# One pass of an FFN: casts put behind each Relu, a PSUM bank of its own for a temporary, an earlier last fold

## The chip, the core and the metric

The kernel runs on one NeuronCore of a Trainium2 chip. Its engines work side by side, each with a queue of its own that it works through in order: TensorE (PE, with its weight loads shown as PEld), VectorE (DVE), ScalarE (ACT), GpSimd (POOL) and SyncE (SP), which here only issues DMAs. Engines wait for one another by semaphores. The metric is the device time of one execution in microseconds. Before the change the median is 775.13 us, from 3 runs between 774.17 and 776.02.

## The reference

Attention with a few sink tokens and a sliding window, then a Fourier mix over tokens and channels, a normalization and a two-layer FFN:

```python
def _attn_ref(q, k, v, n_sink, window):       # B, H, S, D = 4, 8, 768, 64
    scores = scale * np.matmul(q, k.transpose(0, 1, 3, 2))
    keep = is_sink | in_window                # n_sink = 4, window = 128
    scores = np.where(keep, scores, -1000000000.0)
...
    return np.matmul(a, v).astype(np.float32)

def _moe_ref(x, w_ch1, w_ch2):                # x: 4 x 768 x 512
    X = np.fft.fft(np.fft.fft(x, axis=1), axis=2)
    u = x + np.real(X).astype(np.float32)
    un = (u - mu) / np.sqrt(var + 1e-06)      # over the 512 channels
    ch = np.maximum(un @ w_ch1, 0.0) @ w_ch2  # 512 -> 2048 -> 512
    return (u + ch).astype(np.float32)
```

The FFN weights arrive as 64-bit floats.

## The kernel before

**Precision.** Most matmuls of the transform and the FFN take operands split into two parts: a high part, cast to fp32r by ScalarE, and a low part, the difference, made by DVE (from PSUM) or POOL (from SBUF). Three matmuls then stand for one product: high by high, high by low, low by high. So nearly every tile goes through a cast on ACT and a subtraction on another engine before TensorE may use it.

**Attention and transform.** The tokens are 4 batches of 6 blocks of 128. The attention runs in steps, 4 to a block, with the order of each engine written out by hand (SCHEDULE). When the fourth block of a batch is stored, `fourier` registers the events of that batch's transform: for each of three pairs of blocks j, a fold (`fold_n` adds and subtracts the two blocks, `fold_m` folds the channels, `fold_hi` casts on ACT, `fold_lo` subtracts on DVE; lines 349 to 368), then stage 1 on TensorE (`stage1`, L395: tiles za, zr, zb, with cast L400/L402 and subtraction L407/L410), then stage 2 (`stage2a`, L422, copied from PSUM by ACT at L431; `stage2b`, L443, combined by DVE at L448) and the updates of u (L459, L460). The results of the transform go through two PSUM banks in turn, ps_fft ("fft") and, from the start of the FFN on, ps_n ("n"). F_N, F_M and F_S say how many steps after its blocks are stored a fold's parts are issued, S1 how many steps after the last pair the first stage 1 is issued. For the last batch (`tail`) both parts of a fold are on DVE (FOLD_TAIL).

**The first group's FFN.** The 24 blocks form 6 groups of 4. The first group goes through the FFN while the last batch's transform is still running and while the weights are still being prepared, in the loop over f = 0 to 15 (L1256). For each f:

- `ch1` (L656): 12 matmuls of un by w1's f-th slice of 128 columns, into the PSUM tile h; pool ps_h has two buffers of it. The first two ch1 are issued by events at CH1_AT.
- `split` (L1146, L1147): Relu on ACT, which makes the high half of the hidden tile, and the low half on DVE. Both read h.
- `ch2` of f − 1 (L1154): 12 matmuls into the four output banks.
- `convert` of two weight slices (lines 587 to 626), each in three DVE operations that put a 64-bit float together as fp32 (L599, L600, L601), then a cast on ACT and a subtraction on POOL: L610 and L611 for w1 (tiles tw, w_ring), L624 and L625 for w2 (tiles cv, w). The intermediate w of L599 to L601 is the output tile itself in the first 15 conversions, and later a PSUM tile cw in the bank "fft". The raw slices are loaded by SP (L584), three buffers, a load being issued after the conversion that frees its buffer.
- `combine_w1(p)`, every second f: four sums of quarters of w1's p-th pair on POOL (lines 636 to 639, tile tq), and put off to the next f by the list `late`, the function `halves`: two casts on ACT (L643, tile to), each with a subtraction on POOL (L644), and one DMA that writes the pair to w_dram (L645). tq and to have one buffer.
- from f = 6 on, the second group is normalized and turned (`prepare`: L539, L545, L1199, L1227 to L1238).

When the last batch's transform has ended, its SBUF space becomes the pool "wb" for the later w2 slices.

**The main loop.** Groups 1 to 5 then run with w1 products in Strassen's form (`product`, L1320) into the banks A, B and C, and ch2 at L1348. The banks A and C are the tag "h" of ps_h.

**What sets the order.** Up to step 97 (CUT) and again from L1304 the order of each queue is the order of the code. In between, which is the whole stretch around the change, the framework's planner arranges each engine's queue: it goes by the order of the code, by the dependencies and by its own estimates of how long things take. `tc.issue_after(ins)` adds to it that the instructions of the block, where they are on the engine of `ins`, come behind `ins`.

Of the kernel before, what the change touches and what calls it, by code (L numbers as in the profile page):

```python
# [59 lines left out]
FOLD_AT, FOLD_LAST, FOLD_ENG = (0, 4, 8), (0, 4, 8), "VG"  # L60

F_N, F_M, F_S, ROW = (3, 3), (4, 5), (6, 7), (5, 8, 10)
EV_A = 0

SINK0_AT = 3, 3, "V"
# [71 lines left out]
EV_D, EV_Z = 1, 1  # L137
X_AT, X_NOT = (2,), (81, 97)
SOFT_AT = (0, 1, 2, 3)
S1, S2, UD = 7, 1, 2  # L140
FFT_ORDER = (2, 1, 0)
PARTS = {0: ((2,) * 5, 1, 1), 1: ((2,) * 5, 2, 1), 2: ((2,) * 5, 2, 1)}
PARTS_TAIL = ((1,) * 5, 1, 1)
# [61 lines left out]
def kernel(  # L205
# [65 lines left out]
    def run(general):  # L271
        tag = "g" if general else ""
        with ExitStack() as p1:
# [8 lines left out]
            def at(s, eng, fn):  # L282
                ev.setdefault((s, eng), []).append(fn)
# [49 lines left out]
            def fourier(b, at, ready):  # L333
# [30 lines left out]
                def fold_hi(j):  # L364
                    A.copy(gh[:, j], t_["g", j])

                def fold_lo(j):
                    V.tensor_tensor(gl[:, j], t_.pop(("g", j)), f32(gh[:, j]), op=ALU.subtract)
# [97 lines left out]
                for j in range(NHALF):  # L466
                    k = ready[j]
                    e0, e1 = FOLD_TAIL if tail else FOLD_ENG
                    eng = {"V": V, "G": G}
                    at(k + F_N[0], e0, lambda j=j: fold_n(eng[e0], j, 0))  # L470
                    at(k + F_N[1], e1, lambda j=j: fold_n(eng[e1], j, 1))
                    at(k + F_M[0], e0, lambda j=j: fold_m(eng[e0], j, 0))
                    at(k + F_M[1], e1, lambda j=j: fold_m(eng[e1], j, 1))
                    at(k + F_S[0], "A", lambda j=j: fold_hi(j))
                    at(k + F_S[1], "V", lambda j=j: fold_lo(j))
                at(ready[0] + ROW[0], "V", put_row)
                at(ready[0] + ROW[1], "V", mid_sum)
                at(ready[0] + ROW[2], "V", mid_row)
                k = ready[2] + S1
                n1, na, nb = PARTS_TAIL if tail else PARTS[b]  # L480
                for i, (kind, mc) in enumerate((("a", 0), ("a", 1), ("r", 0), ("b", 0), ("b", 1))):
                    n = n1[i]
# [104 lines left out]
            def convert(i, pool=None):  # L587

                which, f = W_ORDER[i]
                r = raw.pop(i)  # L590
                if which == 0:
                    if f % 2 == 0:
                        state["tw"] = npool.tile([P, 2, 512], I32, tag="tw", name=f"tw{f}", bufs=1 if general else 2)
                    t = state["tw"][:, f % 2]
                else:
                    t = npool.tile([P, 512], I32, tag="qs0", name=f"cv{i}", bufs=QSB)

                w = t if "x" not in state else ps_fft.tile([P, 512], I32, tag="fft", name=f"cw{i}", bufs=1)
                V.tensor_scalar(w, r[:, :, 1], 3, 0x3FFFFFF8, op0=ALU.logical_shift_left, op1=ALU.bitwise_and)  # L599
                V.scalar_tensor_tensor(w, r[:, :, 1], -0x40000000, w, op0=ALU.bitwise_and, op1=ALU.bitwise_or)  # L600
                V.scalar_tensor_tensor(t, r[:, :, 0], 29, w, op0=ALU.logical_shift_right, op1=ALU.bitwise_or)  # L601
                load_w(i + LDB)
                tf = t.bitcast(F32)
                if which == 0:
                    if f == 0:
                        state["ring"] = npool.tile([P, 2, 4, 2, 256], F32R, tag="ring", name="w_ring", bufs=1)
                    fb = state["ring"][:, f // 2 % 2]
                    d = [fb[:, 0:2, j] if f % 2 == 0 else fb[:, 3:1:-1, j] for j in range(2)]
                    tf = tf.rearrange("p (h c) -> p h c", h=2)
                    A.copy(d[0], tf)  # L610
                    G.tensor_tensor(d[1], tf, f32(d[0]), op=ALU.subtract)  # L611
                    Wt[f, 0] = [[d[j][:, cc // 2, P * (cc % 2):P * (cc % 2) + P] for cc in range(NCC)] for j in range(2)]
                    if f % 2 == 1:
                        nc.sync.dma_start(w_dram[f // 2][:, 0:3], f32(fb[:, 0:3]).rearrange("p k s c -> p k (s c)"))
                        state["t", f // 2] = state["tw"].bitcast(F32)
                    return
                if NWA <= f < NWA + NHALF:

                    if f == NWA:
                        state["fold"] = [npool.tile([P, NHALF, DM], F32R, tag=t, name=f"w_{t}", bufs=1) for t in ("gh", "gl")]  # L620
                    d = [t[:, f - NWA] for t in state["fold"]]
                else:
                    d = [pool.tile([P, 512], F32R, name=f"w{f}_{j}") for j in range(2)]
                A.copy(d[0], tf)  # L624
                G.tensor_tensor(d[1], tf, f32(d[0]), op=ALU.subtract)  # L625
                Wt[f, 1] = d
# [3 lines left out]
            def combine_w1(p, pool):  # L630

                t = state.pop(("t", p))
                b11, b21, b12, b22 = t[:, 0, :256], t[:, 0, 256:], t[:, 1, :256], t[:, 1, 256:]
                q = pool.tile([P, 4, 256], F32, tag="tq", name=f"tq{p}")
                o = pool.tile([P, 4, 2, 256], F32R, tag="to", name=f"to{p}")
                G.tensor_tensor(q[:, 1], b12, b11, op=ALU.subtract)
                G.tensor_tensor(q[:, 0], b22, q[:, 1], op=ALU.subtract)  # L637
                G.tensor_tensor(q[:, 2], b22, b12, op=ALU.subtract)
                G.tensor_tensor(q[:, 3], b21, q[:, 0], op=ALU.subtract)  # L639

                def halves():
                    for j in (0, 2):
                        A.copy(o[:, j:j + 2, 0], q[:, j:j + 2])  # L643
                        G.tensor_tensor(o[:, j:j + 2, 1], q[:, j:j + 2], f32(o[:, j:j + 2, 0]), op=ALU.subtract)  # L644
                    nc.sync.dma_start(w_dram[p][:, 3:7], f32(o).rearrange("p k s c -> p k (s c)"))  # L645

                late.append(halves)
# [10 lines left out]
                return ps  # L658

            def start_ffn(s):  # L660
                state["h"] = p1.enter_context(tc.tile_pool(name="ps_h" + tag, bufs=2, space=PSUM))
                banks.append((p1.enter_context(tc.tile_pool(name="ps_n" + tag, bufs=1, space=PSUM)), "n", 1))
                for i in range(LDB):
                    load_w(i)
                for i in range(2):
                    at(s + CONV_AT[i], "V", lambda i=i: convert(i))
                for f in range(2):
                    at(s + CH1_AT[f], "T", lambda f=f: hp.append(ch1(0, f, unT0)))
# [474 lines left out]
            g0 = pg.enter_context(tc.tile_pool(name="g0" + tag, bufs=1, side="right"))  # L1143

            def split(h, x):
                A.activation(h[0], x, AF.Relu)  # L1146
                V.scalar_tensor_tensor(h[1], x, 0.0, f32(h[0]), op0=ALU.max, op1=ALU.subtract)  # L1147

            def ch2(f, h, po):
# [102 lines left out]
            hs = {}  # L1252
            for i in (2, 3):
                convert(i, wa)
            combine_w1(0, g0)
            for f in range(NF):  # L1256
                ps = hp.pop(0) if f < 2 else ch1(0, f, unT0)
                hs[f] = [g0.tile([P, 512], F32R, tag=f"h{i}", name=f"h{i}_{f}", bufs=2) for i in range(2)]
                split(hs[f], ps)
                if pw is None:  # L1260
                    do(1)
                if f > 0:
                    ch2(f - 1, hs.pop(f - 1), po)
                for i in range(2 * f + 4, min(2 * f + 6, 2 * NF)):
                    if i % 2 and pw is None:
                        do(1)
                    if W_ORDER[i][0] == 1 and W_ORDER[i][1] == NWA + NHALF and pw is None:
                        while ev:
                            do(1)
                        pf.close()  # L1270
                        pw = p1.enter_context(tc.tile_pool(name="wb" + tag, bufs=1))
                        state["x"] = [pw.tile([P, 7, 512], F32R, name=f"x{i}") for i in range(2)]
                        state["xf"] = pw.tile([P, 2, NCC, 256], F32, name="xf")
                    convert(i, wa if pw is None else pw)
                while late:
                    late.pop()()
                if f % 2 == 1 and f // 2 + 1 < NPR:
                    combine_w1(f // 2 + 1, g0)
                if f == PREP:
                    steps = prepare(1)  # L1280
                for _ in range(PREP_N if f >= PREP else 0):
                    next(steps, None)
# [21 lines left out]
            with tc.manual_schedule():  # L1304
# [51 lines left out]
                for g in range(1, len(groups)):  # L1356
                    steps = prepare(g + 1) if g + 1 < len(groups) else iter(())
                    for it in range(NIT):
# [10 lines left out]
                        ps = {}  # L1369
                        for k in range(7):  # L1370
                            if BANK.index(BANK[k]) == k:
                                pool, t = {"B": banks[it % 2][:2]}.get(BANK[k], (state["h"], "h"))
                                kw = dict(bufs=1) if BANK[k] == "B" else {}
                                ps[BANK[k]] = pool.tile([P, 512], F32, tag=t, name=f"p{BANK[k]}_{g}_{it}", **kw)
                            product(n, ps[BANK[k]])
# [113 lines left out]
```

## Time and profile before

| what | us |
|---|---|
| median of 3 runs | 775.13 (774.17 to 776.02) |
| the profiled execution | 772.87 |
| its span, first to last instruction | 771.1 |
| TensorE busy in the span | 731.0 (95%) |
| DVE busy | 531.6 (69%) |
| POOL busy | 291.5 (38%) |
| ACT busy | 266.5 (35%) |

A timeline row gives start, duration, engine, line, operation, output and inputs with their shapes, how many instructions were merged, and in brackets how long the engine stood idle before it and what ended that. A row of the waits names who waited, for whom, the total in us, how often, and the longest. A busy TensorE is not TensorE at its peak: matmul ends are modelled, and its clock can be granted in part (PEclk). All times count from the start of the span.

### The profile page before, as it was taken

To read this page: it belongs to the slowest core of one execution; us is meant where nothing else is said; L and a number is where in the kernel's file an instruction comes from. 1 tells how busy PE (TensorE), PEld (TensorE's weight loads), DVE (VectorE), ACT (ScalarE), POOL (GpSimd) and SP (SyncE) were. 2 spreads that over 40 slices of the span, in tenths; PEclk is the share of its full clock that TensorE was granted. 3 is DMA by queue.
4 is the path that set the end of the run, shared out by engine and by line. 5 is a ranking of instruction groups with operands and counts; after the bars stand their busy time and mean duration, and the time that the engine had idled before them with its cause. 6 is when DMAs were issued, how large, how long until landed. Compare 5 with 4: busy or idle time off the path is not lost.

```text
span 771.1 us, 13868 instructions
## 1 busy us (share of the span) xinstructions
PE 731.0 (95%) x4899; PEld 624.4 (81%) x4899; DVE 531.6 (69%) x1411; ACT 266.5 (35%) x743; POOL 291.5 (38%) x387
## 2 busy tenths in 40 slices
PE   8999998979879898989999999999999999999996
PEld 6676876757668686868989998998998998898895
DVE  6878578899689887867783677467764778342323
ACT  4787666656632324421103111221122110311110
POOL 2567477478779679650015000520034001500000
PEclk9999999999998999999999999999999999999999
DMA  9763525644404678879655756567555655565601
GB/s 307 255 167 114 154 84 169 195 128 139 164 1 191 229 258 282 281 246 378 218 183 180 256 193 191 177 216 254 171 168 189 218 176 183 183 222 170 190 28 60
DMA packets 84446, 145.90 MB, mean 189 GB/s; under 512 B 7532, under 2 KB 32236, under 8 KB 82960
## 3 DMA queue, kind: packets, MB, share of 16 engines
q1 hardware_dynamic: 84080, 141.17, 56.5%
q0 software_dynamic: 288, 3.76, 1.2%
q8 instruction: 41, 0.67, 0.4%
q14 instruction: 37, 0.30, 0.1%
HBM read 120.77 MB, written 24.13 MB: 188 GB/s over the span
## 4 chain that ended last, share of the span: by engine, by line
PE 54%; POOL 2%; DVE 2%; DMA 2%; issue 1%; ACT 1%; SPq 0%; POOLq 0%; DVEq 0%; ACTq 0%
PE o L1348 29%; PE pB L1320 11%; PE pC L1320 7%; PE pA L1320 7%; DMA wd<-to 1%; POOL to L644 1%; DMA w_b<-wd 1%; PE o L1154 0%; DVE u L1159 0%; DVE x L1238 0%; POOL w_ring L611 0%; PE h L656 0%; POOL w L625 0%; POOL tq L639 0%; POOL tq L637 0%
## 5 line engine op out<-in xcount | busy, mean ns | idle before, releaser
L1348 PE MATMUL o<-w,hring 128*128 128x512 f32 x780 | 192.1, 392 | 0.0
L1348 PEld LDWEIGHTS o<-w,hring 128*128 128x128 f32 x780 | 142.4, 188 | 28.2
L1146 ACT ACTIVATE hring<-tmp 128x512 fp32r<-128x512 f32 x60 | 37.9, 632 | 174.8 <-DVE tmp L1393 84.6
L1227 POOL TENSOR_TENSOR s<-xf 128x512 f32<-128x512 f32 x4 | 5.2, 1294 | 240.3 <-DVE xf L1206 240.3
L1147 DVE SCALAR_TENSOR_TENSOR hring<-tmp,hring 128x512 fp32r<-128x512 f32 x60 | 51.8, 863 | 45.6 <-ACT hring L1146 45.6
L1206 DVE STREAM_TRANSPOSE xf<-un 32x128 f32<-32x128 f32 x256 | 77.4, 302 | 3.5
L764 ACT ACTIVATE sm<-sm,mx 128x132 f32<-128x132 f32 x192 | 75.9, 400 | 3.9 <-DVE mx L758 3.9
L1320 PE MATMUL pB<-x,w_b 128*128 128x256 f32 x456 | 59.4, 279 | 0.8 <-DMA w_b<-wd 0.8
L1320 PEld LDWEIGHTS pB<-x,w_b 128*128 128x128 f32 x456 | 56.6, 188 | 1.8 <-issue 1.0
L739 PE MATMUL s<-ring,q 64*128 64x260 f32 x320 | 49.2, 411 | 8.3 <-DVE mx L758 4.3
L758 DVE CUSTOM_DVE_ANT_0 sm<-s,mask 128x132 f32<-128x132 f32 x192 | 48.4, 292 | 8.0 <-PE s L737 3.2
L1147 DVE SCALAR_TENSOR_TENSOR hring<-pA,hring 128x512 fp32r<-128x512 f32 x20 | 13.8, 691 | 57.0 <-ACT hring L1146 57.0
L656 PE MATMUL h<-un_slots,w_ring 128*128 128x512 f32 x192 | 48.6, 400 | 1.5 <-ACT w_ring L610 0.9
L1146 ACT ACTIVATE hring<-pA 128x512 fp32r<-128x512 f32 x20 | 11.9, 596 | 100.2 <-PE pA L1320 100.2
L739 PEld LDWEIGHTS s<-ring,q 64*128 64x128 f32 x320 | 26.8, 185 | 21.0 <-DVE mx L758 5.3
L656 PEld LDWEIGHTS h<-un_slots,w_ring 128*128 128x128 f32 x192 | 35.7, 190 | 9.6 <-ACT w_ring L610 1.3
L1348 PE MATMUL o<-w_gh,hring 128*128 128x512 f32 x120 | 42.5, 395 | 0.0
L834 PE MATMUL xt<-ptl,ldv 128*64 128x128 f32 x384 | 38.8, 285 | 3.1 <-POOL ptl L812 3.1
L1154 PE MATMUL o<-w,h 128*128 128x512 f32 x156 | 39.3, 400 | 1.3 <-POOL w L625 0.8
L1320 PEld LDWEIGHTS pC<-x,w_b 128*128 128x128 f32 x288 | 36.9, 188 | 2.0
L1320 PE MATMUL pA<-x,w_b 128*128 128x256 f32 x288 | 37.5, 279 | 0.5 <-DMA w_b<-wd 0.5
L803 ACT COPY pta<-pt 128x512 f32<-128x512 f32 x48 | 28.1, 584 | 28.5 <-PE pt L796 28.5
(222 smaller groups left out, 1559.6 us busy)
## 6 DMA issues: line engine op xcount, KB each, us to landing
w_b<-wd SPq DMA_DIRECT2D x172, 256.0 KB, 3.5
w_c<-wd SPq DMA_DIRECT2D x108, 256.0 KB, 3.5
raw<-in_moe_w_ch_dram SPq DMA_DIRECT2D x32, 512.0 KB, 4.7
wd<-to SPq DMA_DIRECT2D x8, 1024.0 KB, 6.7
ldv<-in_v_dram SPq DMA_DIRECT2D x28, 256.0 KB, 3.3
ring<-in_qk_dram SPq DMA_DIRECT2D x24, 264.0 KB, 5.0
wd<-w_ring SPq DMA_DIRECT2D x8, 768.0 KB, 3.9
out_dram<-u SPq DMA_DIRECT2D x24, 256.0 KB, 2.5
```

Of the source, the lines that this page charges most:

```text
L656: T.matmul(ps[:, :tb], a[cc], x[:, :, cc, :], start=n == 0, stop=n == 3 * NCC - 1)
L739: T.matmul(ps[:, j, :P + W], st["q", g][rows, hp, :], keys(g, 2 * hp + j), start=True, stop=True)
L758: V.tensor_tensor_reduce(sm[:, h % 4], ps[:, j, P:P + W], mask[min(qi, 3)], -SCALE, 3.0e38, ALU.add, ALU.min, accum_out=mx[:, 0, h:h + 1])
L764: A.activation(sm[:, h % 4], sm[:, h % 4], AF.Exp, bias=mx[:, 0, h:h + 1], scale=-1.0, accum_out=mx[:, 1, h:h + 1])
L803: A.copy(a, st.pop(("pt", g, hp // 2)))
L834: T.matmul(ps[D * j:D * j + D, p, :], st["v", kb(g) - i][:, h, :], a[:, h % 4, :], start=i == 0, stop=i == n - 1)
L1146: A.activation(h[0], x, AF.Relu)
L1147: V.scalar_tensor_tensor(h[1], x, 0.0, f32(h[0]), op0=ALU.max, op1=ALU.subtract)
L1154: T.matmul(po[i], a[:, ts_], x, start=f == 0 and n == 0, stop=f == NF - 1 and n == 2)
L1206: V.transpose(place[32 * q:32 * q + 32, :, r], un[r].rearrange("p (c q j) -> p c q j", c=NCC, q=4)[:, :, q])
L1320: T.matmul(ps[:, 256 * j:256 * j + 256], w[:, j, a, cs], x[:, xs], start=BANK.index(BANK[k]) == k and j == c == m == 0, stop=j == c == 1 a ...
L1348: T.matmul(po[i], h[:, a, j, ts_], x, start=first and j == m == 0, stop=last and j == 1 and m == 2)
```

## The change

Four things are changed. For the last batch's last fold, the steps of its parts are 1, 1, 2, 2, 3 and 3 after its blocks, instead of 3, 3, 4, 5, 6 and 7, and that batch's stage 1 begins 4 steps after them instead of 7. The conversions' intermediate is always a PSUM tile cw, in a bank of its own; the pool ps_h keeps two banks, so h has one buffer and cw has one. In the main loop, bank A is the one of h and bank C that of cw. The casts of `halves` are put behind the Relu that the code issued last, and `combine_w1(0)` is called at the end of f = 0 instead of before the loop, so that its `halves` come at f = 1.

```diff
+F_LAST = (1, 1), (2, 2), (3, 3)
-S1, S2, UD = 7, 1, 2
+S1, S1_LAST, S2, UD = 7, 4, 1, 2
...
+                    f_n, f_m, f_s = F_LAST if tail and j == NHALF - 1 else (F_N, F_M, F_S)
-                    at(k + F_N[0], e0, lambda j=j: fold_n(eng[e0], j, 0))
+                    at(k + f_n[0], e0, lambda j=j: fold_n(eng[e0], j, 0))
...
-                k = ready[2] + S1
+                k = ready[2] + (S1_LAST if tail else S1)
...
-                w = t if "x" not in state else ps_fft.tile([P, 512], I32, tag="fft", name=f"cw{i}", bufs=1)
+                w = state["h"].tile([P, 512], I32, tag="cw", name=f"cw{i}")
...
                     for j in (0, 2):
-                        A.copy(o[:, j:j + 2, 0], q[:, j:j + 2])
+                        with tc.issue_after(state["relu"]):
+                            A.copy(o[:, j:j + 2, 0], q[:, j:j + 2])
                         G.tensor_tensor(o[:, j:j + 2, 1], q[:, j:j + 2], f32(o[:, j:j + 2, 0]), op=ALU.subtract)
...
-                state["h"] = p1.enter_context(tc.tile_pool(name="ps_h" + tag, bufs=2, space=PSUM))
+                state["h"] = p1.enter_context(tc.tile_pool(name="ps_h" + tag, bufs=1, space=PSUM))
...
-                A.activation(h[0], x, AF.Relu)
+                state["relu"] = A.activation(h[0], x, AF.Relu).ins
...
-            combine_w1(0, g0)
             for f in range(NF):
...
-                if f % 2 == 1 and f // 2 + 1 < NPR:
-                    combine_w1(f // 2 + 1, g0)
+                if f == 0 or f % 2 == 1 and f // 2 + 1 < NPR:
+                    combine_w1((f + 1) // 2, g0)
...
-                                pool, t = {"B": banks[it % 2][:2]}.get(BANK[k], (state["h"], "h"))
+                                pool, t = {"B": banks[it % 2][:2]}.get(BANK[k], (state["h"], {"A": "h", "C": "cw"}.get(BANK[k])))
```

More of the change, by code (lines that the diff above doesn't have):

```diff
@@ L469, in fourier @@
                     eng = {"V": V, "G": G}
-                    at(k + F_N[0], e0, lambda j=j: fold_n(eng[e0], j, 0))
[L471 to L475, printed above, removed]
+                    f_n, f_m, f_s = F_LAST if tail and j == NHALF - 1 else (F_N, F_M, F_S)
+                    at(k + f_n[0], e0, lambda j=j: fold_n(eng[e0], j, 0))
+                    at(k + f_n[1], e1, lambda j=j: fold_n(eng[e1], j, 1))
+                    at(k + f_m[0], e0, lambda j=j: fold_m(eng[e0], j, 0))
+                    at(k + f_m[1], e1, lambda j=j: fold_m(eng[e1], j, 1))
+                    at(k + f_s[0], "A", lambda j=j: fold_hi(j))
+                    at(k + f_s[1], "V", lambda j=j: fold_lo(j))
                 at(ready[0] + ROW[0], "V", put_row)
```

## The prediction

> **What bounds the kernel now.** I read the head of the profile page first, then windows over the stretches, then what TensorE waited for, then the timelines around each wait.
>
> ```profile
> span 771.1 us, 13868 instructions
> ```
>
> ```profile
> 227.00:344.00 117.00, 103.50 (x469) 84.67 (x468) 96.46 (x155) 43.01 (x79) 90.10 (x81) 0.96 0.68 235
> 353.00:756.00 403.00, 403.00 (x2551) 363.52 (x2551) 241.57 (x542) 75.66 (x125) 59.83 (x44) 1.00 0.60 193
> ...
> 227.00:237.00 10.00, 4.38 (x14) 3.70 (x13) 8.18 (x12) 3.86 (x8) 9.92 (x10) 0.66 0.25 105
> 300.00:312.00 12.00, 9.24 (x38) 7.20 (x37) 10.60 (x16) 5.94 (x11) 8.67 (x8) 0.86 0.87 306
> 312.00:344.00 32.00, 29.72 (x129) 23.28 (x128) 24.87 (x37) 12.72 (x23) 21.92 (x20) 1.00 0.73 242
> ```
>
> The columns are the stretch, its length, then the busy time of PE, PEld, DVE, ACT and POOL, the granted clock, the DMA share and GB/s. From 353 to 756 TensorE has no gap at all: 403.00 of 403.00. The change leaves that loop's instructions as they are (its banks A and C get a name each, still one buffer apiece), so it can only be worth what it does before 344: from there on everything moves as one block. Between 227 and 344, the first group's pass through the FFN, TensorE idles 117.00 − 103.50 = 13.5 us, and in two short stretches it was granted 0.66 and 0.86 of its clock. Who ended its waits there:
>
> ```profile
> PE za L395 <- ACT asb L431: 5.4, 1, 5.4
> ...
> PE unt L545 <- ACT xf L1199: 2.8, 1, 2.8
> PE zb L395 <- DVE zr L407: 2.3, 1, 2.3
> PE h L656 <- ACT w_ring L610: 0.9, 1, 0.9
> ...
> PE h L656 <- POOL w_ring L611: 0.6, 1, 0.6
> ...
> PE za L395 <- DVE gl L368: 0.2, 1, 0.2
> ```
>
> Three waits make 5.4 + 2.8 + 2.3 = 10.5 us of it. I look for what stood in front of each in the queue of the engine named.
>
> **First wait, 5.4 us.** TensorE and ScalarE around it:
>
> ```profile
> 226.23 0.89 PE L443 MATMUL b<-cst,zb 128*128 128x258 f32 x6
> 232.55 1.01 PE L395 MATMUL za<-cst,gh 128*128 128x386 f32 x2 [5.43 <-ACT asb L431]
> ...
> 236.50 3.06 PE L1154 MATMUL o<-w,h 128*128 128x512 f32 x12
> 239.40 0.52 PE L395 MATMUL za<-cst,gh 128*128 128x386 f32 x2
> ...
> 241.16 2.91 PE L656 MATMUL h<-un_slots,w_ring 128*128 128x512 f32 x12
> ...
> 223.65 0.62 ACT L643 CAST to<-tq 128x512 fp32r<-128x512 f32 x1 [1.10 <-POOL tq L637]
> 228.39 0.62 ACT L643 CAST to<-tq 128x512 fp32r<-128x512 f32 x1 [4.12 <-POOL tq L639]
> ...
> 231.12 0.62 ACT L365 CAST gh<-f 128x512 fp32r<-128x512 f32 x1 [1.11 <-DVE f L359]
> ...
> 232.13 0.37 ACT L431 COPY asb<-a 128x257 f32<-128x257 f32 x1
> ```
>
> The last matmuls of the earlier batch's transform end at 227.1. The bank they used is free only when ScalarE has copied it (L431), at 232.13. ScalarE was not busy: it stood 4.12 us at a cast of w1's sums (L643) whose input POOL had not finished, then 1.11 us at the cast of the last fold (L365), whose DVE half was itself late. So two items that TensorE does not yet need sit ahead of the one it needs. The idle also cost clock: the stretch's rows run at 0.66. The ten matmuls of one stage 1 part take 236.50 − 232.55 = 3.95 us here, and 241.16 − 239.40 = 1.76 us when warm; less a 0.2 us wait within them (for gl), 2.0 us more are lost. This place is worth up to 5.4 + 0.2 + 2.0 = 7.6 us.
>
> **Second wait, 2.3 us, and third, 2.8 us.**
>
> ```profile
> 251.46 0.62 ACT L643 CAST to<-tq 128x512 fp32r<-128x512 f32 x1 [5.29 <-POOL tq L637]
> 253.59 0.62 ACT L643 CAST to<-tq 128x512 fp32r<-128x512 f32 x1 [1.50 <-POOL tq L639]
> 254.12 0.47 ACT L400 CAST zr<-zr 1x386 fp32r<-1x386 f32 x1
> ...
> 301.99 1.14 ACT L643 CAST to<-tq 128x512 fp32r<-128x512 f32 x2 [2.48 <-POOL tq L639]
> ...
> 303.56 0.57 ACT L1199 COPY xf<-unt 128x512 f32<-128x512 f32 x1
> ...
> 304.19 0.66 PE L545 MATMUL unt<-ident,un 128*128 128x128 f32 x4 [2.75 <-ACT xf L1199]
> 304.60 2.53 PE L656 MATMUL h<-un_slots,w_ring 128*128 128x512 f32 x6
> ...
> 310.41 0.60 PE L545 MATMUL unt<-ident,un 128*128 128x128 f32 x4
> ...
> 316.72 3.00 PE L656 MATMUL h<-un_slots,w_ring 128*128 128x512 f32 x12
> ...
> 322.31 2.93 PE L656 MATMUL h<-un_slots,w_ring 128*128 128x512 f32 x12
> ```
>
> Both times the same cast again stands in front of what TensorE waits for (L400, whose DVE half L407 follows; L1199). The third also costs clock: the 18 matmuls from 304.60 to 310.41 take 5.81 us, while the 24 from 316.72 to 322.31 take 5.59, or 4.19 for 18: 1.6 us lost. The second is worth up to 2.3, the third up to 2.8 + 1.6 = 4.4.
>
> **The change, part by part.**
>
> *Casts behind Relu.* The two L643 casts of a pair, of 0.62 us each, are held behind the Relu of the f last traced, and pair 0 is built one f later. What is moved with them: two POOL subtractions (L644) and one DMA on SP (L645) per pair. Four of POOL's sums (L636 to L639) move for pair 0 only. By the time a Relu has run, POOL's sums are mostly ready, so the casts should wait little and leave L431, L400 and L1199 free. First place: I take 6.5 of 7.6, together with the fold below. Second: 1.5 of 2.3, since DVE's half still has its own queue. Third: 3.0 of 4.4, since the second transpose also needs its input from DVE (L539), which came at 301.48 to 302.22, 2 us after the first. Sum 11.0, bounds 0 and 14.3.
>
> ```profile
> 301.48 0.74 DVE L539 TENSOR_SCALAR un<-u,stat 128x512 f32<-128x512 f32 x1
> ```
>
> Cost: L643 now waits for TensorE through Relu, and behind it POOL's L644, L625 and L611, and on SP the weight loads behind L645. The weights so made are used one or more f later, 5.6 us each (322.31 − 316.72); I take 0, and if that cover is gone it is the 0.6 to 0.9 us of the w_ring rows, once for each f where it happens.
>
> *Last fold and transform 2 to 4 and 3 steps sooner.* Four DVE operations, one cast and one DVE subtraction are only reordered; FOLD_TAIL keeps both halves on DVE, so POOL gets nothing new. It removes the 1.11 us wait of L365 and the 0.2, counted in the 6.5. The transform's six stores, on SP among the weight loads, come sooner too; a load that then stands behind one is late by the store's issue, part of the small waits above, and I take 0.
>
> *The conversion's temporary in a bank of its own.*
>
> ```profile
> L599 DVE TENSOR_SCALAR cw<-raw x17: 679/694/697, 279.3 to 333.6; 128x512 int32<-128x512 int32 x17
> ...
> L599 DVE TENSOR_SCALAR cv<-raw x7: 410/421/1485, 182.2 to 263.4; 128x512 int32<-128x512 int32 x7
> ...
> L600 DVE SCALAR_TENSOR_TENSOR cw<-raw,cw x17: 675/695/697, 280.2 to 337.4; 128x512 int32<-128x512 int32 x17
> L600 DVE SCALAR_TENSOR_TENSOR tw<-raw,tw x8: 668/680/809, 132.5 to 262.0; 128x512 int32<-128x512 int32 x8
> L600 DVE SCALAR_TENSOR_TENSOR cv<-raw,cv x7: 679/1216/1369, 182.9 to 264.3; 128x512 int32<-128x512 int32 x7
> ```
>
> 15 conversions (7 cv, 8 tw) worked in SBUF, 17 in PSUM (cw: min/median/max in ns). Moving the 15 costs 15 × (694 − 421) = 4.1 us of DVE at L599. It may return 7 × (1216 − 695) = 3.6 at L600, the cv rows having been stretched beside a busy POOL. Net 0.5 us of DVE, bounds −3 and +4. [...] What the bank buys: the first cw starts at 279.3 because the transform held the shared bank until then; with its own bank, conversions can begin in DVE's idle time before.
>
> *ch1's bank alone.* That bank is taken from ch1: h has one buffer, so ch1 of f+1 waits until Relu and L1147 of f have read it. The cover is ch2 of f−1, 5.59 / 2 = 2.8 us (for f = 0 it is what the earlier transform has left).
>
> ```profile
> 320.24 0.60 ACT L1146 ACTIVATE h<-h 128x512 fp32r<-128x512 f32 x1
> ...
> 322.83 0.68 DVE L1147 SCALAR_TENSOR_TENSOR h<-h,h 128x512 fp32r<-128x512 f32 x1
> ```
>
> Here the reader is done at 323.51, and the next ch1 began at 322.31: with one bank a stall of 1.2 us. Without queueing, Relu 0.6 and L1147 0.7 fit in 2.8 with 1.5 to spare, so the stall comes only where DVE or ACT lags by two operations. Bounds: 0, and 15 hand-offs × 1.2 = 18. I take two such stalls, 2.5 us, near the end that the rows favour, since the lags behind L643 go.
>
> **Sum.** −11.0 + 2.5 + 0.5 = −8.0; I give back 0.5 as DVE must follow. DVE was busy 96.46 of 117 us, 82%; if the stretch shrinks by 7.5 it is 88%, which is what it reached in 300 to 312 (10.60 of 12.00). More would need a fuller DVE than this stage shows. Span 771.1 − 7.5 = 763.6. The profiled execution took 772.87 us, and the median of the runs is 775.13, or 4.0 above the span; so 767.6 us.
>
> **Rivals.**
> 1. *DVE is the bound.* The waits vanish and come back as waits for w_ring and w (0.9 and 0.6 already there). For: 88% at 300 to 312. Against: 20.5 us of DVE idle in 227 to 344. Gain 0 to 4: 771 to 775.
> 2. *The single h bank, on the other side.* If L1147 ends over 2.8 us after ch1's end on most f, each of 15 hand-offs stalls about 1 us: +15 against −11, so +4: 779. It decides from about 0.7 us a hand-off. For: the 1.2 us above. Against: most of DVE's lag is queueing that the planner reorders.
> 3. *The clock.* Small stalls at every hand-off might drop the granted clock. In 227 to 237 it fell after a 5.4 us idle. Against: in 312 to 344, where TensorE idled 2.3 us in waits of under 1 us, the clock stayed at 1.00. If it did drop to 0.86 over 60 us of matmuls: 60 / 0.86 − 60 = +9.8, less the gain of 7.5: 777.4. [...]
> 4. *All of it.* Waits and clock loss go and no bank stall comes: −13, 762.
> 5. *It does nothing it says:* the planner had the casts behind Relu in effect, or conversions still wait for space. Then 775.
>
> **How the numbers follow.** Forecast (764 to 771.5) 0.52; full gain 0.07; DVE-bound with a small gain 0.12; within 0.2% (1.55 us, about what a measurement can tell from no change; rivals 1 and 5) 0.11; single bank 0.15; clock 0.03. Faster 0.71, same 0.11, slower 0.18. The range runs from 761.5, the full gain, to 777.5, into the single bank's cases, which leaves out some 0.15.
>
> **What would show it.** Right: no L643 ahead of L431, L400 and L1199 with a wait; PE's waits at za, zb and unt below 1 us each; no stretch at 0.66; first cw for the second half of the pairs well before the transform's end; the loop's first product at about 337 instead of 344.80.
>
> ```profile
> 344.80 1.58 PE L1320 MATMUL pA<-x,w_c 128*128 128x256 f32 x12
> ```
>
> Wrong: rows "PE h L656 <- DVE h L1147" adding up to more than 5 us; waits for w_ring or w above 4; DVE under 85% busy with TensorE still waiting.

## The result and the profile after

| | before | after |
|---|---|---|
| median, us (4 runs each) | 775.58 (774.17 to 777.71) | 766.39 (766.02 to 766.73) |
| ratio, 95% interval | 1 | 0.9879 (0.9855 to 0.9903) |
| the profiled execution / its span, us | 772.87 / 771.1 | 766.28 / 764.6 |

The forecast was 767.6 us. The number came out; the account of it did not. The gain is 9.2 us in the medians and 6.5 us in the two profiled spans: before's profiled execution lies 2.7 us below this median, after's 0.1. The two traces account for the 6.5 alone; the rest goes along with the mean granted clock, which was 0.980 to 0.992 in 50 further executions of before (spans from 778.8 us at 0.981 to 770.9 at 0.992), 0.992 in the profiled one, and 0.991 to 0.996 in after's four, and no trace shows in which stretch.

The prediction cut the span at fixed times. Those cut different work once anything has moved, so here both spans are cut at the same instructions: a store of the attention near 120 us (`u<-x,mx`), the last transpose `pk` of the sink rows, which ends the attention for TensorE, and the first product `pA` of the main loop. I call the first part the *head*, the second the *stage*. Windows of before, then of after (columns as in the prediction; the last row of after is the main loop):

```profile
120.05:215.06 95.01, 84.29 (x739) 66.93 (x737) 81.66 (x279) 57.74 (x204) 65.62 (x110) 1.00 0.50 161
215.06:344.80 129.74, 116.25 (x553) 95.61 (x552) 109.05 (x174) 46.81 (x87) 98.09 (x89) 0.96 0.62 214
```

```profile
120.52:208.82 88.30, 83.76 (x738) 67.15 (x737) 72.57 (x261) 56.22 (x201) 57.26 (x108) 1.00 0.40 126
208.82:337.99 129.17, 117.12 (x554) 95.15 (x552) 114.17 (x191) 48.78 (x90) 94.22 (x91) 0.97 0.71 249
337.99:764.60 426.61, 418.04 (x2641) 376.66 (x2639) 251.20 (x560) 77.72 (x128) 59.75 (x44) 0.99 0.59 192
```

The head is 6.7 us shorter, the stage 0.6, the main loop as long as before (771.1 − 344.80 = 426.3). The prediction placed all 7.5 us of its gain in the stage. Its window 227 to 344 would seem to bear it out:

```profile
227.00:344.00 117.00, 108.34 (x514) 88.55 (x513) 99.76 (x168) 44.08 (x80) 85.24 (x82) 0.99 0.81 283
227.00:237.00 10.00, 10.00 (x53) 9.22 (x52) 8.97 (x18) 4.62 (x9) 7.41 (x9) 1.00 0.64 213
...
312.00:344.00 32.00, 27.89 (x131) 21.70 (x130) 23.89 (x36) 8.78 (x15) 16.02 (x14) 0.95 0.80 277
```

TensorE's idle time there is down from 13.5 to 8.7 us and the slow stretch at 227 is gone. But this window now holds 6 us of the main loop, and what stood in it first has moved out on the left. Cut by landmarks, TensorE idles 12.0 us of the stage against 13.5 before.

**The head.** What TensorE waited for there, before and then after:

```profile
PE xt L834 <- POOL ptl L812: 3.1, 1, 3.1
PE s L739 <- DVE mx L758: 3.1, 7, 1.1
PE a L422 <- DVE d L449: 1.8, 2, 1.0
```

```profile
PE s L742 <- DVE mx L761: 1.0, 5, 0.2
...
PE a L423 <- DVE d L450: 0.8, 1, 0.8
```

Three waits lost 3.1, 2.1 and 1.0 us: 6.2 of the 6.7. The first, on POOL's queue in before:

```profile
200.62 0.34 POOL L776 TENSOR_TENSOR sk<-sm,sk 128x32 fp32r<-128x32 f32 x1
200.93 5.88 POOL L611 TENSOR_TENSOR w_ring<-tw,w_ring 128x512 fp32r<-128x512 f32 x4
206.76 0.63 POOL L812 TENSOR_SCALAR_AFFINE_SELECT ptl<-pta 128x512 f32<-128x512 f32 x1
```

Four subtractions of converted w1 slices stand in front of the attention's mask, and TensorE waits for the mask. In after TensorE has no wait for `ptl` in the head. The other two waits are for DVE, which in before also worked on conversions during the attention: the group rows of L599, the first operation of each conversion, in the head are

```profile
L599 DVE TENSOR_SCALAR tw<-raw 128x512 int32<-128x512 int32 x4 | 3.3, 823 | 0.0
...
L599 DVE TENSOR_SCALAR cv<-raw 128x512 int32<-128x512 int32 x3 | 1.3, 423 | 0.0
```

and in after

```profile
L601 DVE TENSOR_SCALAR cw<-raw 128x512 int32<-128x512 int32 x2 | 1.4, 684 | 0.0
```

Seven conversions in the head before, two after, and these late, as DVE's timeline of after shows:

```profile
198.04 0.69 DVE L601 TENSOR_SCALAR cw<-raw 128x512 int32<-128x512 int32 x1
```

The reason is in the code: the bank of cw belongs to the pool ps_h, which is opened when the attention gives up its score banks. Before, the early conversions needed no bank, and the planner put them into the attention's queues wherever their data had come. So the edit of the bank acts as a gate, where the prediction had it open a gate. The run e4 below tests this.

**The stage.** TensorE's waits from 185 to 355 in after:

```profile
PE h L659 <- DVE h L1150: 7.2, 6, 2.3
PE za L396 <- DVE gl L369: 2.3, 1, 2.3
PE b L444 <- DVE d L450: 1.1, 1, 1.1
...
PE o L1157 <- POOL w L627: 0.5, 1, 0.5
...
PE zb L396 <- DVE zb L411: 0.2, 1, 0.2
...
PE h L659 <- POOL w_ring L613: 0.2, 1, 0.2
```

The three waits of 5.4, 2.8 and 2.3 us are down to 2.3 (for another engine), none and 0.2. The prediction had them go; that the casts are not alone in this is seen in e1 below. In their place stand 7.2 us at the one bank of h. And the stage has taken over five conversions from the head: DVE is busy 114.17 of 129.17 us, 88%, against 84% before.

### The profile page after: what moved, and what is told of

Read it like the earlier page. It is cut to its first block, busy times and chain, and to the rows that moved or that the text cites. A ratio compares the mean times of both kernels' runs of the same rounds, so it can differ in the third digit from the quotient of the medians.

```text
span 764.6 us, 13878 instructions
## 1 busy us (share of the span) xinstructions
PE 729.8 (95%) x4899; PEld 622.5 (81%) x4899; DVE 528.8 (69%) x1411; ACT 267.1 (35%) x743; POOL 279.1 (37%) x387
## 4 chain that ended last, share of the span: by engine, by line
PE 72%; DVE 12%; POOL 5%; issue 3%; ACT 2%; DMA 2%; SPq 1%; ACTq 0%; DVEq 0%; POOLq 0%
PE o L1350 29%; PE pB L1322 11%; PE pC L1322 7%; PE pA L1322 7%; PE xt L837 4%; PE s L742 4%; PE pt L799 2%; PE za L396 2%; PE h L659 2%; PE zb L396 1%; DVE sm L761 1%; PE o L1157 1%; DVE cw L602 1%; DVE cw L601 1%; DVE s L748 1%
## 5 line engine op out<-in xcount | busy, mean ns | idle before, releaser
L1150 DVE SCALAR_TENSOR_TENSOR hring<-tmp,hring 128x512 fp32r<-128x512 f32 x60 | 51.8, 864 | 45.6 <-ACT hring L1149 45.6
L659 PE MATMUL h<-un_slots,w_ring 128*128 128x512 f32 x192 | 50.6, 412 | 7.4 <-DVE h L1150 7.2
L1150 DVE SCALAR_TENSOR_TENSOR hring<-pA,hring 128x512 fp32r<-128x512 f32 x20 | 13.8, 692 | 56.4 <-ACT hring L1149 56.4
L1322 PE MATMUL pC<-x,w_b 128*128 128x256 f32 x288 | 37.4, 279 | 0.0
```

The lines of the kernel that those rows point to most:

```text
L659: T.matmul(ps[:, :tb], a[cc], x[:, :, cc, :], start=n == 0, stop=n == 3 * NCC - 1)
L1322: T.matmul(ps[:, 256 * j:256 * j + 256], w[:, j, a, cs], x[:, xs], start=BANK.index(BANK[k]) == k and j == c == m == 0, stop=j == c == 1 a ...
```

## The experiments

Theories at the start. *One:* casts and fold give the gain in the stage, as predicted. *Two:* keeping the conversions out of the attention gives it. Head and stage are cut as above, from one profiled execution each; times are the medians, ratios are to before as it ran beside each set of runs (medians 775.46 to 776.07).

| run | head | stage | DVE busy in stage | median | ratio (95%) |
|---|---|---|---|---|---|
| before | 95.0 | 129.7 | 109.1 | 775.58 | 1 |
| after: bank, casts, fold | 88.3 | 129.2 | 114.2 | 766.39 | 0.9879 (0.9855–0.9903) |
| e1: bank | 88.4 | 133.6 | 115.9 | 771.04 | 0.9944 (0.9920–0.9967) |
| e4: hold | 88.3 | 143.8 | 130.2 | 781.62 | 1.0081 (1.0041–1.0121) |
| e5: casts, fold | 95.0 | 131.6 | 114.7 | 777.19 | 1.0018 (0.9998–1.0038) |
| e6: hold, casts, fold | 88.4 | 145.0 | 129.0 | 782.45 | 1.0097 (1.0059–1.0136) |
| e7: bank, casts | 88.3 | 131.6 | 115.0 | 769.30 | 0.9915 (0.9894–0.9935) |
| e8: bank, fold | 88.3 | 131.8 | 115.8 | 768.40 | 0.9924 (0.9900–0.9949) |
| e9: after, first 15 conversions in SBUF | 96.4 | 137.0 | 113.2 | 784.65 | 1.0125 (1.0105–1.0145) |
| b1: after, second bank for h | 88.3 | 130.2 | 114.2 | 770.02 | 0.9921 (0.9904–0.9937) |
| e10: e6, all conversions in SBUF | 88.3 | 156.8 | 146.3 | 797.92 | 1.0286 (1.0257–1.0315) |
| e11: casts | 95.0 | 128.5 | 111.5 | 772.97 | 0.9961 (0.9938–0.9983) |
| e12: fold | 96.5 | 136.3 | 119.8 | 781.03 | 1.0067 (1.0045–1.0089) |
| b2: after, prepare's casts behind Relu | 88.4 | 129.7 | 113.1 | 767.71 | 0.9888 (0.9863–0.9913) |

Ahead of the head, where the first conversion has not yet begun in any run, the traces differ by up to 3.7 us (the store stood at 119.8 in e11, at 120.5 in after, at 123.4 in b2), so the medians tell more of the whole, head and stage more of the place.

**The bank alone, and the gate alone.** e1 is before with the bank's edits only:

```diff
-                w = t if "x" not in state else ps_fft.tile([P, 512], I32, tag="fft", name=f"cw{i}", bufs=1)
+                w = state["h"].tile([P, 512], I32, tag="cw", name=f"cw{i}")
...
-                state["h"] = p1.enter_context(tc.tile_pool(name="ps_h" + tag, bufs=2, space=PSUM))
+                state["h"] = p1.enter_context(tc.tile_pool(name="ps_h" + tag, bufs=1, space=PSUM))
...
-                                pool, t = {"B": banks[it % 2][:2]}.get(BANK[k], (state["h"], "h"))
+                                pool, t = {"B": banks[it % 2][:2]}.get(BANK[k], (state["h"], {"A": "h", "C": "cw"}.get(BANK[k])))
```

> The bank alone: every conversion's temporary in a PSUM bank of its own, ch1 with one buffer; casts, sums and fold as before. Theory 1 (mine on record: the gain is the casts' and the fold's waits, the bank costs): no gain, ratio 1.000 to 1.005. Theory 2 (from the trace after: the changed kernel is 6.8 us ahead already at the last block of the attention, because without the early tile the planner can no longer put 7 conversions into the attention's DVE and POOL queues): 6 to 7 us ahead at the first ch1, then part of it lost again to the waits of casts and bank; ratio 0.990 to 0.998.

e4 is before with the gate only; the conversions keep their old tiles, but DVE's first operation of each comes behind the last block of the attention that the code had stored by then:

```diff
+                hold = state.get("stored")
+                with tc.issue_after(hold) if hold is not None else ExitStack():
+                    V.tensor_scalar(w, r[:, :, 1], 3, 0x3FFFFFF8, op0=ALU.logical_shift_left, op1=ALU.bitwise_and)
...
+                        state["stored"] = V.tensor_tensor(u[Q_BLOCKS[g % NB]].rearrange("p (h d) -> p h d", h=H), st.pop(("x", g)),
```

> Before, with one edit: the DVE operations of the conversions are queued behind the last store of an attention block that the code had issued, so none can go into the attention's queue earlier; bank, casts and fold as before. Theory 1: nothing, or up to 2 us slower as that work now falls into the first group's pass (ratio 1.000 to 1.003). Theory 2: the first ch1 comes 5 to 7 us sooner; if the waits behind the casts stay as they are the whole comes to 0.991 to 0.997.

Both heads are 88.3 to 88.4: the 6.7 us come from either gate, so theory two holds for the head, and e1's 0.9944 lies in its range. But its price for e4, a gain, missed: the stage grew by 14.0 us, and the kernel lost 0.8%. In e1 it grew by 3.9. TensorE's waits in e1 are, among others,

```profile
PE h L656 <- DVE h L1147: 5.1, 6, 2.3
PE za L395 <- ACT asb L431: 3.3, 1, 3.3
...
PE unt L545 <- DVE un L539: 0.3, 1, 0.3
```

There is none at zb for `zr`. So the prediction's second and third waits go with the bank alone, with the casts where they were, and the first is down to 3.3 us.

Both stages hold the delayed conversions. DVE's group rows for them show the difference, first in the stage of e4, then of e10 (an experiment further down) between 208.5 and 352 us, then in the stage of after (count, then busy us and mean ns):

```profile
L602 DVE SCALAR_TENSOR_TENSOR cv<-raw,cv 128x512 int32<-128x512 int32 x7 | 7.9, 1145 | 0.0
L601 DVE TENSOR_SCALAR cv<-raw 128x512 int32<-128x512 int32 x7 | 7.6, 1097 | 0.0
L602 DVE SCALAR_TENSOR_TENSOR tw<-raw,tw 128x512 int32<-128x512 int32 x7 | 6.2, 890 | 0.0
```

```profile
L605 DVE SCALAR_TENSOR_TENSOR cv<-raw,cv 128x512 int32<-128x512 int32 x14 | 18.0, 1288 | 0.1
L604 DVE SCALAR_TENSOR_TENSOR tw<-raw,tw 128x512 int32<-128x512 int32 x15 | 16.1, 1070 | 0.2
```

```profile
L602 DVE SCALAR_TENSOR_TENSOR cw<-raw,cw 128x512 int32<-128x512 int32 x30 | 20.6, 688 | 0.4
```

In these rows the operation with both inputs in SBUF (SCALAR_TENSOR_TENSOR) takes 890 to 1288 ns on average, with POOL busy 72% of e4's stage and 73% of e10's; the last operation of a w1 slice, not shown, takes 742 and 873. With one input in PSUM it is 688, and the prediction's tw rows of before have a median of 680 in SBUF. New theories: the bank saves this stretching (*contention*), or it lets the conversions begin before the transform frees its bank (*early start*).

**The gate with casts and fold, and these without the bank.** e5 has casts and fold on before's banks:

```diff
+F_LAST = (1, 1), (2, 2), (3, 3)
...
+                k = ready[2] + (S1_LAST if tail else S1)
...
+                        with tc.issue_after(state["relu"]):
+                            A.copy(o[:, j:j + 2, 0], q[:, j:j + 2])
...
+                if f == 0 or f % 2 == 1 and f // 2 + 1 < NPR:
+                    combine_w1((f + 1) // 2, g0)
```

> Casts behind Relu and earlier last fold, without the bank: ch1 keeps two buffers, the temporary stays in the output tile and later in the transform's bank. Theory 1: the three waits of 10.5 us go and no bank stall comes, ratio 0.985 to 0.990, the first ch1 at its old time of 220 us. Theory 2: only what the stage itself gives, as the attention's end is not helped: 0.992 to 0.997.

e6 has e5's lines and e4's:

> Casts behind Relu, earlier last fold, and the conversions held out of the attention; no bank change, ch1 with two buffers. Theory 1: as the casts and fold alone, 0.985 to 0.990. Theory 2: the two gains add, as DVE allows: first ch1 at 213 us and no waits on ch1's buffer, ratio 0.980 to 0.986, below the changed kernel's 0.988.

e5 gives no gain (1.0018, outside the ranges of both theories), so theory one falls. Why the first wait did not go is seen on ScalarE and DVE of e5:

```profile
223.65 0.60 ACT L1149 ACTIVATE h<-h 128x512 fp32r<-128x512 f32 x1
231.13 0.62 ACT L366 CAST gh<-f 128x512 fp32r<-128x512 f32 x1 [6.88 <-DVE f L360]
231.65 0.59 ACT L1149 ACTIVATE h<-h 128x512 fp32r<-128x512 f32 x1
232.14 0.37 ACT L432 COPY asb<-a 128x257 f32<-128x257 f32 x1
```

```profile
221.74 2.41 DVE L353 TENSOR_TENSOR f<-us,us 128x512 f32<-128x512 f32 x2
...
224.73 1.55 DVE L460 TENSOR_TENSOR u<-u,d 128x257 f32<-128x257 f32 x1
...
227.07 1.49 DVE L363 TENSOR_TENSOR f<-f 128x255 f32<-128x255 f32 x1
...
229.62 1.48 DVE L360 TENSOR_TENSOR f<-f 128x255 f32<-128x255 f32 x1
```

The cast of the sums no longer stands there, and ScalarE waits 6.88 us one item later, at the cast of the fold. The copy L432 runs at 232.14 as it did in before (232.13), and TensorE waits 5.1 us for it, before 5.4. What holds it is DVE's half of the fold, which ends at 231.1 in both. DVE is busy without a gap from 221.74 to 231.10 here, and the fold's two operations of 128x255 take 1.49 and 1.48 us, in before 0.85 and 0.88; in after they took 0.95 and 0.40:

```profile
219.69 0.95 DVE L363 TENSOR_TENSOR f<-f 128x255 f32<-128x255 f32 x1
...
221.21 0.40 DVE L360 TENSOR_TENSOR f<-f 128x255 f32<-128x255 f32 x1
```

POOL subtracts three w2 slices (L627) between 224.7 and 230.8 us in e5; between 213 and 222 in after it subtracts none, as the conversions come later there. That these slow the fold is likely and was not tested.

e6 missed its expectation, a gain, by far (1.0097): casts and fold do not make up for the 14 us that the gated conversions cost in SBUF.

**Which half goes with the bank.** e7 leaves the fold out of the change, e8 the casts:

```diff
-                k = ready[2] + (S1_LAST if tail else S1)
+                k = ready[2] + S1
```

> The change without the earlier fold: bank and casts. With the bank alone at 0.994 and the whole change at 0.988, this and the next run share out the missing 0.6%. Theory A, the casts carry it: 0.988 to 0.990, and the bank-alone run's wait of 3.3 us at za for ACT's asb goes. Theory B, the fold carries it, since with the casts alone (and two buffers) the wait at za stayed and was held by the fold's cast: 0.992 to 0.995, the wait at za stays at 3 us.

```diff
-                        with tc.issue_after(state["relu"]):
-                            A.copy(o[:, j:j + 2, 0], q[:, j:j + 2])
+                        A.copy(o[:, j:j + 2, 0], q[:, j:j + 2])
```

> The change without the casts behind Relu: bank and earlier fold. Theory A (casts carry the rest): 0.993 to 0.995. Theory B (the fold does): 0.988 to 0.990.

Both runs lie between the two theories (0.9915 and 0.9924), so neither half is it alone: from e1's stage of 133.6 the casts take 2.0, the fold 1.8, both 4.4. In e7 the wait at za for `asb` is gone, 3.3 us in e1, but the waits at h are 7.1 us in place of 5.1. The window of e1's stage:

```profile
208.99:342.58 133.59, 120.45 (x553) 96.79 (x552) 115.91 (x191) 48.82 (x90) 95.89 (x91) 0.95 0.67 241
```

TensorE was busy 120.45 us of it and idle 13.1, in after 117.12 and 12.0. The matmuls are the same, so by these windows about 3.3 of the 4.4 us are matmuls at a better clock (0.95 to 0.97) and only 1.1 is idle time.

**The change with SBUF conversions.** e9 keeps casts, fold and one bank for h, but lets the first 15 conversions work in their output tile again:

```diff
-                w = state["h"].tile([P, 512], I32, tag="cw", name=f"cw{i}")
+                w = t if "x" not in state else state["h"].tile([P, 512], I32, tag="cw", name=f"cw{i}")
```

> The whole change, but the first 15 conversions work in their output tile again, as before, so that the planner may put them into the attention; the later ones have the bank of their own, ch1 one buffer. Theory 2: the 6.7 us at the attention's end are lost (first ch1 at 220 us), while the stage keeps what the bank gives it, namely that conversion 15 need not wait for the transform's bank; ratio 0.994 to 1.000. Rival: the keeping out is all there is, and without it one buffer costs 5 to 7 us: 1.005 to 1.010. Rival on record (theory 1: casts and fold give the gain): 0.988 as the change.

It was 1.25% slower than before, worse than either theory had it. The head's gain is gone, which confirms the gate, and TensorE waits long at the one bank of h:

```profile
PE h L659 <- DVE h L1150: 15.6, 7, 4.9
```

The sum is that of the prediction's second rival (+15), in 7 waits instead of 15. Against e5, which has two banks, the stage is only 5.4 us longer. DVE also stands 10.1 us there waiting for raw slices, in after 3.1 and in e5 3.9, so how much of the 5.4 is the bank's and how much the late slices' stays open.

**The second bank back.** b1 is after, and ch1 of odd f from 7 on uses the transform's bank, free by then:

```diff
-                ps = state["h"].tile([P, 512], F32, tag="h", name=f"h_{g}_{f}")
+                if "x" in state and f % 2:
+                    ps = ps_fft.tile([P, 512], F32, tag="fft", name=f"h_{g}_{f}", bufs=1)
+                else:
+                    ps = state["h"].tile([P, 512], F32, tag="h", name=f"h_{g}_{f}")
```

> The whole change, and ch1 of every second f puts its result into the bank of the transform once that has ended (from f = 7 on), so that ch1 has two banks again for the second half. Price of the single buffer: of the 7.2 us that ch1 waits for DVE in the changed kernel, four waits lie there, 1.49 + 0.79 + 2.30 + 0.54 = 5.1 us, and 1.7 us of slow clock behind the longest. If the single buffer is what costs them: 3 to 6 us faster than the changed kernel, ratio to before 0.980 to 0.985. If DVE is the bound there (the waits come back as waits for w_ring and w): within 1 us of it, 0.987 to 0.990.

```profile
PE o L1160 <- POOL w L627: 3.0, 2, 2.2
PE h L662 <- DVE h L1153: 2.7, 3, 1.2
PE h L662 <- ACT w_ring L612: 2.4, 1, 2.4
```

The waits for h fell from 7.2 to 2.7 us and came back as 5.4 us for weights. The stage did not shrink (130.2), and the kernel was not faster but 0.4% slower than after, with intervals that just fail to meet; 0.9921 lies outside both ranges expected. In the one trace 1.0 us of it is in the stage, and 2.2 lie ahead of the head, where no edited line has run; the mean granted clock of that execution was 0.983, in after 0.992. So the waits at h are where TensorE meets a chain of DVE, ACT and POOL that is itself late, much as the first rival has it.

**Contention or early start.** e10 is e6, with every conversion in SBUF to its end; none waits for a bank:

```diff
-                w = t if "x" not in state else ps_fft.tile([P, 512], I32, tag="fft", name=f"cw{i}", bufs=1)
+                w = t
```

> As the run with hold, casts and fold (stage of 145.0 us from the last sink transpose of the attention to the first product), but the temporary is always the output tile in SBUF, so that conversion 15 does not wait for the transform's bank either; ch1 keeps two buffers. It tells apart what the bank gives inside the stage (hold alone 143.8, bank alone 133.6). Early start of the later conversions: the stage falls to 129 to 134, ratio 0.988 to 0.994. Contention: with the temporary in SBUF, L600 and L601 read two SBUF operands beside POOL, all 32 times now; the stage stays at 140 or more, L600 of the cv rows keeps its median of 1.1 us or more, ratio 1.003 to 1.010.

```profile
208.39:365.14 156.75, 125.86 (x554) 98.98 (x552) 146.29 (x194) 48.81 (x91) 114.91 (x92) 0.91 0.57 201
```

Free to start, and yet the stage grew by another 11.8 us against e6, with DVE busy 93% of it. Contention had the sign right, and the size was well beyond what I had expected. Its rows above tell how: 1070 and 1288 ns.

**Casts alone, fold alone.** e11 and e12 are before with one of the two sets of lines of e5:

> Casts behind Relu alone. Theory 1 as on record: the second and the third wait (2.3 and 2.8 us) go and most of the first, 0.987 to 0.992. After the run of casts and fold without the bank (1.002): the first wait stays, because the last fold's cast, with 6.9 us behind DVE, then holds the ACT queue; stage within 2 us of 129.7, ratio 0.998 to 1.003.

> The earlier last fold and transform alone. If DVE's slow fold is what ends the first wait (operations of 1.2 to 1.6 us beside POOL instead of 0.4 to 0.7), issuing it sooner gains up to 2 us there: 0.997 to 1.000. If its queue only changes places with other DVE work: 1.000 to 1.003.

The casts alone gain a little (0.9961, between the two ranges expected), with the stage 1.2 us shorter. The second and third waits are gone there too (0.3 us left at zb), but TensorE waits 2.7 us for `w_ring` and 2.3 us for the hidden tile instead. The fold alone loses (1.0067, outside both ranges), with the stage 6.6 us longer and the head 1.5, as in e9; the head's waits are those of before, and the mean granted clock of that execution was 0.986, in before 0.992. TensorE's longest waits in e12's stage are

```profile
PE za L396 <- ACT asb L432: 4.9, 1, 4.9
PE unt L547 <- ACT xf L1201: 3.5, 1, 3.5
```

so the first wait stays, and the third, at xf, is even longer. Why an earlier fold costs so much without the gate stays open: the planner orders the whole stretch anew, and I did not separate that.

**One more cast behind Relu.** b2 is after, with the casts of the second group's sums put behind Relu as well:

```diff
-                    A.copy(hi, x)
+                    with tc.issue_after(state["relu"]) if n == 1 else ExitStack():
+                        A.copy(hi, x)
```

> The whole change, and the casts of the second group's preparation (x, from sums of the turned tiles) also put behind the Relu last issued. The longest wait left in the changed kernel, 2.30 us before ch1 of f = 14, follows a Relu that stood behind such casts. If TensorE's waits are the bound: 2 to 4 us faster than the changed kernel, 0.983 to 0.986. If DVE is the bound, as the two-bank run says: within 1.5 us of it, 0.986 to 0.990.

No change that can be told from after (0.9888 and 0.9879, intervals overlapping). The run fits "DVE is the bound" and does not show it: two of the casts still run ahead of the Relu in question (at 317.70 and 319.41 us, the Relu at 319.93), and the wait aimed at is still 2.52 us long. In after, that Relu has ended at 317.69, and DVE works off six other operations before it comes to the low half (L1150) at 321.33. No run put the low half ahead of them, so the order of DVE's queue stands beside its load as a cause of these waits. No run had a lower median than the changed kernel.

## Why the number was right and the account wrong

| term of the stage's sum, us | forecast | measured | by |
|---|---|---|---|
| casts and fold | −11.0 | −4.4 | e1 to after, stage |
| own bank and single h bank | +3.0 | +3.9 | before to e1, stage |
| given back, as DVE must follow | +0.5 | in the above | |
| attention ahead of the stage | not looked at | −6.7 | e1, e4, head |
| sum | −7.5 | −7.2 | |

The two spans differ by 6.5 us, since some 0.7 go the other way ahead of the head and in the main loop; the medians differ by 9.2.

- **The step that failed** is the choice of the stretch. The prediction wrote that the change "can only be worth what it does before 344", which holds, and then read only 227 to 344. The largest term lies in the attention, ahead of 215: the change alters what the planner may place there. A row in the prediction itself showed it: tw conversions from 132.5 us on, amid the attention.
- **Casts and fold** were sized at 11.0 of 14.3 and gave 4.4, and that only beside the bank: on before's banks the same lines made the stage 1.9 us longer (e5). The rows named what stood in front in ScalarE's queue, but an item removed is worth only the distance to the next late one. For the first wait that was the fold's cast, whose DVE half was late by itself; the prediction named it and still took 6.5 of 7.6 us. In e5, without the bank, that wait stayed whole (5.1 us). The second and third waits left with the casts alone (e11) and with the bank alone (e1), and other waits came in their place.
- **The conversions' bank** was priced on its operations alone (+0.5 of DVE, bounds −3 and +4), and "conversions can begin in DVE's idle time" was named as its use. Little of that start came: the 16th conversion, the first that in before waits for the transform's bank (279.3 us), began at 269.9 in after, 9.4 us sooner, of which 6.2 are the earlier begin of the stage. Its effects are the gate (6.7 us) and less stretching (688 ns in the rows above in place of 890 to 1288). With the conversions held out of the attention, the stage costs 143.8 us with them in SBUF and 133.6 in the bank, 10.2 less, although e1 also has the single h bank.
- **The single h bank**: 2.5 us forecast, 7.2 us of waits in after. The sign set for it, over 5 us, did show; but by b1 they are not this bank's price, since the stage is no shorter with most of them gone.
- **The first rival** (DVE the bound) fits what is seen inside the stage: DVE is 88% busy, as much as the prediction's sum allowed it, and what is taken off TensorE's waits reappears (e7, e11, b1). It is not shown, since DVE's order was not tested. **The clock** stayed: 0.96 before and 0.97 after in the stage, with two drops in after, to 0.66 from 222 to 227 and from 322 to 327, each behind an idle of 2.30 us.
- **Of the other signs**, these came as set: the stretch at 0.66 from 227 to 237 is gone (though 222 to 227, behind the wait at za, and 322 to 327, behind the longest idle at h, run at 0.66 in after); the first product at 337.99 against 337; and the casts behind Relu, with no wait above 0.21 us:

```profile
228.52 0.60 ACT L1149 ACTIVATE h<-h 128x512 fp32r<-128x512 f32 x1 [2.69 <-PE h L659]
229.01 1.13 ACT L646 CAST to<-tq 128x512 fp32r<-128x512 f32 x2
```

The wait at za came out at 2.3 us where under 1 was set. The conversions of the second half of the pairs were to begin well before the transform's end; the first of them began at 273.8 us, after its last update of u (272.5). Two errors of opposite sign, −6.7 unseen and 6.6 too much for casts and fold, cancelled: that the number came out is luck.

## What to carry to other kernels

Cut two traces at the same instructions, not at the same times, and price each piece before believing that a gain sits where the edit is. Where a planner orders the queues, a new buffer or bank is also a gate: ask which instructions could start early before and cannot now, and in whose queues they stood. If VectorE combines two SBUF tiles beside a busy GpSimd, try one of them in PSUM (here 688 ns in place of 890 to 1288), and expect a removed wait to be worth only the distance to the next late input.

## What was not expected of the hardware

DVE's operation on two SBUF tiles of 128x512 int32 took 890 to 1288 ns on average in the rows shown, beside a POOL busy some 72% of the stage, and 688 with one of the two in PSUM. The tensor_scalar from SBUF to SBUF, with one input, was stretched too: a mean of 1097 ns over the seven of w2 slices in e4, where the seven in before have a median of 421. The seven L600 of w2 slices in before took 1.22 to 1.37 us in four cases, all beside a POOL operation, and 0.68 to 0.70 in three, two of them beside one too. So a POOL at work goes with the stretching and does not settle it; that POOL is its cause is my reading, and no run changed POOL's work alone.

The idles at the single h bank cost clock only once:

```profile
275.09 3.01 PE L659 MATMUL h<-un_slots,w_ring 128*128 128x512 f32 x12 [1.49 <-DVE h L1150]
...
311.67 2.93 PE L659 MATMUL h<-un_slots,w_ring 128*128 128x512 f32 x12
...
322.16 4.49 PE L659 MATMUL h<-un_slots,w_ring 128*128 128x512 f32 x12 [2.30 <-DVE h L1150]
```

After 2.30 us of idling the 12 matmuls took 4.49 us in place of 2.93, and the clock from 322 to 327 was 0.66; after 1.49 us they took 3.01, and after the other four idles (0.54 to 1.15 us) 3.01 to 3.04. In e9 they took 3.03 us after an idle of 1.23, and 5.49 after one of 4.91. So the clock fell after one of after's six idles at h, the longest. The length of the idle alone does not tell it: after's wait of 2.30 us at za was followed by 0.66 from 222 to 227, and in before an idle of 2.29 us at zb by 1.00 from 255 to 260.
